# Loading the x tiles one stream at a time over 128 partitions, with new task lists

## The chip, the cores and the metric

The kernel runs on one core of one Trainium2 chip. The metric is device time in microseconds of one execution, without the host. The kernel before takes 252.27 us as the median of three runs (251.86 to 256.15). Lower is better.

A core has five engines that run side by side, each with its own instruction list: TensorE (PE in the profile, its weight loads PEld), VectorE (DVE), ScalarE (ACT), GpSimd (POOL) and SyncE (SP, which here only issues DMAs). DMAs are carried by 16 DMA engines, which all issuing engines share. Matmuls write to PSUM, which has 8 banks.

## The reference

One transformer layer in two halves, for one sequence of 2048 tokens with 448 features, in bfloat16.

```
h  = x + A(layernorm(x))
h2 = h + B(layernorm(h))

A: q,k,v = x @ wqkv, 16 heads of 28; each token attends to 8 keys,
   at distances 0, 2, 4, ... 14 before it; softmax; then @ wo
B: z = gelu(x @ w_in), split in z1 and z2 (896 each)
   g = w_sp @ layernorm(z2) + b_sp        (w_sp is 2048 x 2048)
   (z1 * g) @ w_out
```

## The kernel before

**Streams and tiles.** The 2048 tokens are cut into two streams of 1024 tokens, and the streams lie one over the other: a matmul with 64 rows serves stream 0, its partner in the other half of the array serves stream 1. For the attention, x is loaded in 9 tiles per stream. Tile i begins at token 114 i - 16 of its stream, so neighbouring tiles overlap by 14 tokens: the attention's look-back then stays inside a tile. Each tile has 128 tokens, the 64 even ones in partitions 0 to 63 and the 64 odd ones in partitions 64 to 127, since the attention looks back in steps of two. The first 16 tokens of tile 0 in stream 0 lie before the sequence and are set to zero.

**Where things lie.** The x tiles (`xs`) and the staged q weights share one buffer with a later stage; in the profile they are called z2p. The staged k and v weights lie in w_in. The padded copies of the q and k weights, the k and q results and several other tiles are views of `reg1`, `reg2`, `reg3`, which the profile shows as reg.

**Stages on TensorE.** First 15 matmuls on constant data, then transposes of the first tiles, q and k for tile 0 and for tile 1 (chunks 0 and 1), then tiles 2 to 4 together (chunk 2) and 5 to 8 together (chunk 3), with v, the logits, the row sums and the weighted sums of each tile in between; then the output projection (`mmy`), z2 and z1, and from about 132 us on the large product with w_sp (L1052) and the last product (L1081).

**A tile's way to TensorE.** Two loads; statistics on VectorE (`bn1`, lines 656 and 657, one pair of instructions per stream); the inverse deviation on ScalarE or GpSimd (`rs1`); normalization on VectorE (`nrm1`, line 674); then a transpose. Tiles 0 to 2 are transposed on TensorE (`tT1`), tiles 3 to 8 by a DMA (`tD1`, line 680) that SyncE issues.

**The loads.** Tile i is loaded by two DMAs, `xs i_0` for the even and `xs i_1` for the odd tokens (line 540). Each writes 64 partitions and takes both streams at once; tile 0 needs four smaller ones (lines 544 and 546). The source view has 64 rows outermost, then the two streams. The q, k and v weights come in four pieces each (line 559); q is copied by `cpq`, k by `cpk` into the padded form that the matmuls read. The loads of tiles 2 to 8 also wait until all four q pieces have landed (lines 587 to 589).

**What sets the order.** Every piece of work is a task with a modelled duration, dependencies and buffers. `SEQ` at the top of the file holds five lists of task numbers, one per engine, found beforehand by a search; `Planner.replay` walks them with the modelled durations, picks PSUM banks and buffers as it goes and emits the instructions in that order. At run time an engine runs its list strictly in order and waits on semaphores where the data needs it. So a modelled duration has no force at run time: it only decides which bank or buffer a task gets.

On SyncE the list of the kernel before begins with xs1_0, the pieces of tile 0, two q pieces, pieces of k and of the wo padding; then eight x loads; then the two large v pieces (wv0, wv1), more x loads and the transposes of tiles 3 and 4. ScalarE issues xs1_1, two q pieces, one k piece and one piece that serves k and v.

The functions that the change touches, with what calls them:

Of the kernel before, what the change touches and what calls it, by code (L numbers as in the profile page):

```python
# [6 lines left out]
D = 448  # L7
DH = 28
FH = 896
# [4 lines left out]
ST = 1024  # L14
# [20 lines left out]
SEQ = (  # L35
# [29 lines left out]
)  # L65
# [154 lines left out]
class Planner:  # L220
# [68 lines left out]
    def replay(self, t0=0.7):  # L289
# [13 lines left out]
        for _ in tasks:  # L303
# [34 lines left out]
            if t.nbytes:  # L338
                dma_free = max(dma_free, now + 0.3) + t.nbytes / t.bw / 1000.0
                t.end = dma_free + t.setup  # L340
                self.landed = max(self.landed, t.end)
            else:
                t.end = now + dur + extra
# [11 lines left out]
def bass_sequential_preLN__sliding_local_dilated__mixer_gmlp__prompt_kernel(  # L355
# [18 lines left out]
    with contextlib.ExitStack() as top:  # L374
# [101 lines left out]
        kv_old = r_wl["k"] + r_wl["v"]  # L476
        stg_old = r_wl["q"] + [r for i in range(NT) for s in range(2) for r in r_xs[i][s]]
        reg2_old = [r for rr in r_q + r_k for r in rr] + [r_qend]
# [26 lines left out]

        def dma(eng, name, fn, nbytes, deps=(), reads=(), writes=(), rel=(), store=False, issue=0.5, bw=245.0, after=(), setup=2.0):
            def em():
                rd = list(reads)
                for w in t.waits:
                    if w.nbytes:  # L510
                        rd.append(w.mark)
                    else:
                        rd += w.mark
                key, n = iss(eng, fn, reads=rd, writes=writes, prod="dma", inc=16, after=after)
                t.mark = Res("mark")
                t.mark.writes = {key: n}
                if store:
                    sch.store_keys.append(key)
            t = add(name, eng, issue, em, deps=deps, rel=rel, nbytes=nbytes)
            t.bw = bw  # L520
            t.setup = setup
            return t
# [10 lines left out]

        t_xs = [[] for _ in range(NT)]
        XT = X.rearrange("(s t) f -> t s f", s=2)

        def ld_xs(i, w, eng):
            lo = TQ * i - HALO + w
            if i:
                t_xs[i].append(dma(eng, "xs%d_%d" % (i, w), lambda e: e.dma_start(  # L540
                    xs[64 * w:64 * w + 64, i, :, :], XT[lo:lo + 127:2, :, :]), 128 * D * 2,
                    writes=[r_xs[i][0][w], r_xs[i][1][w]]))
                return
            t_xs[0].append(dma(eng, "xs0a_%d" % w, lambda e: e.dma_start(
                xs[64 * w + HALO // 2:64 * w + 64, 0, 0, :], X[w:w + 111:2, :]), 56 * D * 2, writes=[r_xs[0][0][w]]))
            t_xs[0].append(dma(eng, "xs0b_%d" % w, lambda e: e.dma_start(  # L546
                xs[64 * w:64 * w + 64, 0, 1, :], X[ST + lo:ST + lo + 127:2, :]), 64 * D * 2, writes=[r_xs[0][1][w]]))
        t_w = {}
# [7 lines left out]
        def ld_w(p, n, eng):  # L556
            c0 = "qkv".index(p[0]) * D
            dst, src = halves(w_st[p], A_wqkv[:, c0:c0 + D * len(p)])[n]
            t = dma(eng, "w%s%d" % (p, n), lambda e: e.dma_start(dst, src),
                    (64 if n > 1 else 384) * len(p) * D * 2, writes=[r_wl[x][n] for x in p], bw=200.0 if n > 1 else 330.0)  # L560
            for x in p:
                t_w.setdefault(x, []).append(t)
# [3 lines left out]
        def ld_win(z, deps, after=()):  # L566
            for n, (dst, src) in enumerate(halves(w_in[z], B_w_in[:, FH * z:FH * z + FH])):
                t = dma("sp", "win%d_%d" % (z, n), lambda e, dst=dst, src=src: e.dma_start(dst, src),
                        (64 if n > 1 else 384) * FH * 2, deps=deps, writes=[r_win[z][n]], bw=200.0 if n > 1 else 330.0, after=after)
                t_win.setdefault(z, []).append(t)  # L570
# [13 lines left out]
        for i in range(2, NT):  # L584
            ld_xs(i, 0, "sp")
            ld_xs(i, 1, "sp")
            for t in t_xs[i]:
                t.deps += t_w["q"]
                t.waits += t_w["q"]
        for n in range(4):  # L590
# [44 lines left out]
        def ln_unit(u, which, src_deps, after_h=()):  # L635
# [18 lines left out]
            for n in range(2):  # L654
                def em(n=n):
                    iss("dve", lambda e: e.bn_stats(st[n], src[n]), reads=rsrc[n], writes=[rl[n]])  # L656
                    iss("dve", lambda e: e.bn_aggr(mv[n], st[n]), reads=[rl[n]], writes=[rl[n]])  # L657
                tb.append(add("bn%d_%d_%d" % (which, u, n), "dve", 0.76, em, deps=src_deps))

# [26 lines left out]
            def em_t():  # L686
                o = bk[0] * 1024
                for c in range(NC7):
                    iss("pe", lambda e, c=c: e.transpose(psb[:, o + 128 * c:o + 128 * c + 128],
                                                        tring[:, h[0], 128 * c:128 * c + 128], ident[:, :]),  # L690
                        reads=r_tr[h[0]] + [r_ident], writes=[r_bank[bk[0]]])
            tt = add("tT%d_%d" % (which, u), "pe", 0.9 if u < 2 else 0.5, em_t, deps=tn + [c_ident], acq=[("ps", 1, bk)],
                     rel=[("tr", h)], mode="F", nmm=7)
# [10 lines left out]
        for i in range(NT):  # L704
            t_xh.append(ln_unit(i, 1, t_xs[i] + ([c_x0] if i == 0 else [])))

# [233 lines left out]
        for u in range(NU):  # L940
# [18 lines left out]
            t_h.append(th)  # L959
            t_hT.append(ln_unit(u, 2, [th]))  # L960
            tb3 = []
# [193 lines left out]
```

## Time and profile before

The profile is one execution on the chip, and its rows give microseconds.

| | |
|---|---|
| time, median of three runs | 252.27 us (251.86 to 256.15) |
| the profiled execution's own time | 255.13 us |
| its span, first to last instruction | 253.4 us |
| TensorE matmul, busy | 237.7 us (94%) |
| VectorE, busy | 138.3 us (55%) |
| ScalarE, busy | 86.7 us (34%) |
| GpSimd, busy | 23.4 us (9%) |
| mean clock granted to TensorE | 0.987 |
| moved by DMA | 25.62 MB, mean 101 GB/s |

How to read it: a row of a group names the line of the kernel, the engine, the operation, and the tiles written and read; then the count, the busy time, and the idle time before it with what ended it. "PE psum L802" is a matmul of line 802 that writes PSUM. A q or SPq names a queue or a DMA issue. In the views by time, the first number is the start in the span and the second the length. In a table of windows, the columns are the busy time of each engine, then the granted clock of TensorE, the mean busy share of the DMA engines, and GB/s.

### The profile page before, as it was taken

How to read it: one execution, taken by the hardware profiler on the slowest of the kernel's cores; microseconds unless marked ns; L12 is line 12 of the kernel's file. 1: busy time of each engine (PE TensorE's matmuls, PEld its weight loads, DVE VectorE, ACT ScalarE, POOL GpSimd, SP SyncE). 2: the span in 40 equal slices, each digit the busy share in tenths (PEclk: the TensorE clock that was granted, in tenths of full speed). 3: DMA queues.
4: the chain of work that ended last, by engine and by line, in shares of the span. 5: the costliest groups of instructions: out<-in, count | busy, mean ns of one | idle time of the engine just before them, and what ended most of it. 6: DMA issues, size and time to landing. Idle time of an engine off the chain costs nothing.

```text
span 253.4 us, 6573 instructions
## 1 busy us (share of the span) xinstructions
PE 237.7 (94%) x2942; PEld 119.5 (47%) x2952; DVE 138.3 (55%) x278; ACT 86.7 (34%) x110; POOL 23.4 (9%) x61
## 2 busy tenths in 40 slices
PE   7674999987999899999999999999999999999995
PEld 2372665544455454454444444444444444444443
DVE  3585975569599898769881005105700238321573
ACT  2543968676597834857571000000000000000000
POOL 7010200000030203203450000000000000000000
PEclk9997999999799999999999999999999999999999
DMA  5879987568863997695733363310000000010213
GB/s 153 238 189 203 259 97 184 81 106 117 171 169 54 209 221 180 120 131 119 160 84 85 83 153 79 77 26 0 3 0 0 18 0 21 0 36 0 75 36 110
DMA packets 60657, 25.62 MB, mean 101 GB/s; under 512 B 48084, under 2 KB 60484, under 8 KB 60628
## 3 DMA queue, kind: packets, MB, share of 16 engines
q1 hardware_dynamic: 59524, 24.22, 46.1%
q10 hardware_dynamic: 1104, 0.98, 1.4%
q8 instruction: 23, 0.38, 0.6%
q14 instruction: 6, 0.05, 0.1%
HBM read 11.75 MB, written 1.84 MB: 54 GB/s over the span
## 4 chain that ended last, share of the span: by engine, by line
PE 87%; DMA 5%; SPq 4%; issue 3%; DVE 0%
PE psum L1052 38%; PE psum L1081 8%; PE psum L1015 8%; PE psum L768 8%; PE psum L968 7%; PE psum L802 6%; PE psum L948 5%; PE psum L835 3%; SPq L540 3%; PE psum L891 2%; DMA z2p<-in_A_wqkv_dram 2%; DMA xh<-tring 2%; DMA w_in<-in_A_wqkv_dram 1%; PE psum L868 1%; SPq L546 1%
## 5 line engine op out<-in xcount | busy, mean ns | idle before, releaser
L1061 DVE TENSOR_TENSOR ub<-psum,reg 128x512 bf16<-128x512 f32 x28 | 18.8, 687 | 58.5 <-PE psum L1052 40.3
L1052 PE MATMUL psum<-reg,z2p 128*128 128x512 bf16 x219 | 49.2, 379 | 0.3
L1052 PE MATMUL psum<-wspT_lo,z2p 128*128 128x512 bf16 x219 | 48.7, 379 | 0.4 <-issue 0.2
L1052 PEld LDWEIGHTS psum<-wspT_lo,z2p 128*128 128x128 bf16 x224 | 21.8, 98 | 26.5 <-DVE z2p L998 0.4
L1052 PEld LDWEIGHTS psum<-reg,z2p 128*128 128x128 bf16 x224 | 21.8, 98 | 26.5 <-DVE ub L1061 0.4
L768 PE MATMUL psum<-xh,reg 64*128 64x114 bf16 (+3 forms) x448 | 27.2, 271 | 1.1 <-DVE reg L628 1.0
L968 PE MATMUL psum<-w_in,xh 64*128 64x448 bf16 x224 | 22.6, 349 | 0.4 <-DMA xh<-tring 0.4
L1081 PE MATMUL psum<-reg 128*128 128x448 bf16 (+1 forms) x119 | 22.3, 342 | 0.0
L1015 PE MATMUL psum<-xh,w_in 64*128 64x512 bf16 x196 | 22.0, 376 | 0.0
L626 ACT ACTIVATE reg<-psum 128x896 bf16<-128x896 f32 (+4 forms) x24 | 17.8, 758 | 11.0 <-PE psum L802 5.5
L1091 DVE TENSOR_TENSOR tring<-psum,x_tm 128x448 bf16<-128x448 f32 (+1 forms) x17 | 9.8, 594 | 21.1 <-PE psum L1081 21.1
L768 PEld LDWEIGHTS psum<-xh,reg 64*128 64x128 bf16 x448 | 16.3, 93 | 9.9 <-DVE reg L628 1.2
L802 PE MATMUL psum<-w_in,xh 64*128 64x448 bf16 x126 | 15.8, 398 | 4.3 <-issue 4.2
L984 DVE BATCH_NORM_STATS2 st<-z2p 128x6 f32<-128x448 bf16 x32 | 17.5, 611 | 3.2 <-ACT z2p L978 3.2
L850 ACT ACTIVATE reg<-psum 128x928 bf16<-128x928 f32 x18 | 16.4, 943 | 5.4 <-PE psum L835 5.2
L978 ACT ACTIVATE z2p<-psum 128x896 bf16<-128x896 f32 x16 | 13.9, 917 | 9.9 <-PE psum L968 6.5
L1025 ACT ACTIVATE reg<-psum 128x1024 bf16<-128x1024 f32 x14 | 13.9, 1029 | 7.9 <-PE psum L1015 7.9
L1081 PEld LDWEIGHTS psum<-reg 128*128 128x128 bf16 x119 | 11.5, 98 | 10.3 <-DVE tring L1091 0.4
L968 PEld LDWEIGHTS psum<-w_in,xh 64*128 64x128 bf16 x224 | 10.6, 94 | 11.2 <-DMA xh<-tring 0.8
L1015 PEld LDWEIGHTS psum<-xh,w_in 64*128 64x128 bf16 x196 | 9.5, 94 | 11.4
L631 POOL TENSOR_SCALAR rs<-mv 128x2 f32<-128x2 f32 x18 | 5.1, 284 | 105.0 <-DVE mv L657 86.0
L656 DVE BATCH_NORM_STATS2 st<-z2p 128x6 f32<-128x448 bf16 x18 | 11.0, 612 | 6.9 <-DMA z2p<-in_A_x_dram 6.8
(54 smaller groups left out, 202.8 us busy)
## 6 DMA issues: line engine op xcount, KB each, us to landing
w_in<-in_B_w_in_dram SPq DMA_DIRECT2D x4, 672.0 KB, 5.5
x_tm<-in_A_x_dram SPq DMA_DIRECT2D x4, 448.0 KB, 5.2
z2p<-in_A_x_dram SPq DMA_DIRECT2D x15, 112.0 KB, 3.3
out_dram<-tring SPq DMA_DIRECT2D x15, 112.0 KB, 1.8
w_in<-in_A_wqkv_dram SPq DMA_DIRECT2D x3, 336.0 KB, 5.8
reg<-in_A_wo_dram SPq DMA_DIRECT2D x4, 196.0 KB
reg<-in_B_w_out_dram SPq DMA_DIRECT2D x1, 784.0 KB, 5.6
reg<-in_B_b_sp_dram SPq DMA_DIRECT2D x1, 512.0 KB, 4.8
```

The costliest lines, as they stand in the source:

```text
L626: iss("act", lambda e: e.activation(dst, src, AF.Copy), reads=rd, writes=wr)
L768: iss("pe", lambda e, c=c, s=s, gi=gi, lhs=lhs, mov=mov: e.matmul(psum[:, bk[s] * 512 + cw * gi:bk[s] * 512 + cw * gi + cw], lhs, mov, sta ...
L802: iss("pe", lambda e, c=c, s=s: e.matmul(psum[:, bk[s] * 512:bk[s] * 512 + D], xh[64 * s:64 * s + 64, BLK[s][c], 128 * i:128 * i + 128], w ...
L850: iss("act", lambda e: e.activation(E[:, es[0], 2 * n:2 * n + 2, :], pair_view(lb, 0, 8 * JW), AF.Exp, scale=SCALE), reads=[r_bank[lb[0]], ...
L968: iss("pe", lambda e, c=c, s=s: e.matmul(psum[:, zb[s] * 512:zb[s] * 512 + D], xh[64 * s:64 * s + 64, BLK[s][c], 128 * u:128 * u + 128], w ...
L978: iss("act", lambda e: e.activation(z2p[:, u:u + 9:8, D * k:D * k + D], pair_view(zb, 0, D), AF.Gelu_apprx_tanh), reads=[r_bank[zb[0]], r_ ...
L984: iss("dve", lambda e, b=b: e.bn_stats(st3[:, b, k, :], z2p[:, b, D * k:D * k + D]), reads=[r_z2[b][k]], writes=[r_st3[b][k]])
L1015: iss("pe", lambda e, c=c, s=s: e.matmul(psum[:, bk[s] * 512:bk[s] * 512 + 512], w_in[0][64 * s:64 * s + 64, c, 128 * f:128 * f + 128], xh ...
L1025: iss("act", lambda e: e.activation(z1p[f].rearrange("p (s t) -> p s t", s=2)[:, :, 512 * ch:512 * ch + 512], pair_view(bk, 0, 512), AF.Ge ...
L1052: iss("pe", lambda e, b=b: e.matmul(psum[:, gb[0] * 512:gb[0] * 512 + 512], z2p[:, b, 128 * f:128 * f + 128], src[:, b, 512 * (tc % 2):512 ...
L1061: iss("dve", lambda e: e.tensor_tensor(ub[:, us_[0], :], psum[:, gb[0] * 512:gb[0] * 512 + 512], bb[:, 512 * tc:512 * tc + 512], ALU.add), ...
L1081: iss("pe", lambda e, f=f: e.matmul(psum[:, wb[0] * 512 + d0:wb[0] * 512 + d1], z1p[f][:, 128 * m:128 * m + 128], w_out[:, f, d0:d1], star ...
```

## The change

1. `ld_xs(i, n, eng)` now loads tile i of one stream n as one DMA over all 128 partitions. The source is a view that puts the parity w outermost (2), then the 64 rows of that parity. Tile 0 of stream 0, whose first rows are missing, is still loaded in two parts of 56 partitions. There are 17 full loads of 112 KB and these two parts, instead of 16 of 112 KB and four parts.
2. The loads of tiles 2 to 8 no longer wait for the q weights.
3. The statistics of one stream depend on that stream's load alone.
4. The model's constants change (issue of a DMA 0.62 instead of 0.5, all loads at 285 GB/s, start of a DMA 0.4, and others), and with them the five lists. There is one task less, so every number after it is shifted by one.

By name, SyncE now issues xs0_1, xs0_0b, xs1_0, xs0_0a, wk0, wop1, wkv3, wq3, xs2_1, xs2_0, wop0, xs3_1, wq1, wop2, xs4_1, wop3, xs3_0, xs4_0, wv1, wv0, xs8_1, xs8_0, xs6_0, xs7_0, xs5_1, xs7_1, xs6_1, then the transposes of tiles 4 and 3, then xs5_0 (here the second digit is the stream). ScalarE issues xs1_1, wkv2, wq2 and wk1, then runs rs1_1, then issues wq0. TensorE does k of tiles 1 and 0 first, then the transpose of tile 2, then q of tiles 0 and 1, then v of tiles 0, 2 and 1, the logits of tile 0, and chunk 2. VectorE takes the statistics of all loads in a new order; those of tile 6, stream 1 stand in its list ahead of the normalization of tile 6 and of `mask0`.

```diff
-        t_xs = [[] for _ in range(NT)]
-        XT = X.rearrange("(s t) f -> t s f", s=2)
-
-        def ld_xs(i, w, eng):
-            lo = TQ * i - HALO + w
-            if i:
-                t_xs[i].append(dma(eng, "xs%d_%d" % (i, w), lambda e: e.dma_start(
-                    xs[64 * w:64 * w + 64, i, :, :], XT[lo:lo + 127:2, :, :]), 128 * D * 2,
-                    writes=[r_xs[i][0][w], r_xs[i][1][w]]))
-                return
...
+        t_xs = [[[], []] for _ in range(NT)]
+
+        def ld_xs(i, n, eng):
+            lo = ST * n + TQ * i - HALO
+            if lo >= 0:
+                parts = [(xs[:, i, n, :], X[lo:lo + 128, :].rearrange("(j w) f -> w j f", w=2))]
+            else:
+                parts = [(xs[64 * w + HALO // 2:64 * w + 64, i, n, :], X[w:w + 111:2, :]) for w in range(2)]
+            for k, (dst, src) in enumerate(parts):
+                t = dma(eng, "xs%d_%d%s" % (i, n, "ab"[k] if len(parts) > 1 else ""), lambda e, dst=dst, src=src: e.dma_start(dst, src),
+                        128 * D * 2 // len(parts), writes=[r_xs[i][n][k]] if len(parts) > 1 else r_xs[i][n], bw=285.0)
+                t_xs[i][n].append(t)
...
             ld_xs(i, 0, "sp")
             ld_xs(i, 1, "sp")
-            for t in t_xs[i]:
-                t.deps += t_w["q"]
-                t.waits += t_w["q"]
...
-                tb.append(add("bn%d_%d_%d" % (which, u, n), "dve", 0.76, em, deps=src_deps))
+                tb.append(add("bn%d_%d_%d" % (which, u, n), "dve", 0.77, em, deps=src_deps[n]))
...
-            t_xh.append(ln_unit(i, 1, t_xs[i] + ([c_x0] if i == 0 else [])))
+            t_xh.append(ln_unit(i, 1, [t_xs[i][0] + ([c_x0] if i == 0 else []), t_xs[i][1]]))
```

More of the change, by code (lines that the diff above doesn't have):

```diff
@@ L338, in replay @@
             if t.nbytes:
-                dma_free = max(dma_free, now + 0.3) + t.nbytes / t.bw / 1000.0
+                dma_free = max(dma_free, now + 0.4) + t.nbytes / t.bw / 1000.0
                 t.end = dma_free + t.setup
@@ L476, in bass_sequential_preLN__sliding_local_dilated__mixer_gmlp__prompt_kernel @@
         kv_old = r_wl["k"] + r_wl["v"]
-        stg_old = r_wl["q"] + [r for i in range(NT) for s in range(2) for r in r_xs[i][s]]
+        stg_old = r_wl["q"] + [r for i in range(NT) for rr in r_xs[i] for r in rr]
         reg2_old = [r for rr in r_q + r_k for r in rr] + [r_qend]
@@ L504, in dve4x, with dma @@
             return (190.0 + 0.26 * n) / 1000.0
-        def dma(eng, name, fn, nbytes, deps=(), reads=(), writes=(), rel=(), store=False, issue=0.5, bw=245.0, after=(), setup=2.0):
+        def dma(eng, name, fn, nbytes, deps=(), reads=(), writes=(), rel=(), store=False, issue=0.62, bw=285.0, after=(), setup=2.0):
             def em():
@@ L532, in ld_x @@
                 t_x[b] = t
-        t_xs = [[] for _ in range(NT)]
-        XT = X.rearrange("(s t) f -> t s f", s=2)
-        def ld_xs(i, w, eng):
-            lo = TQ * i - HALO + w
-            if i:
-                t_xs[i].append(dma(eng, "xs%d_%d" % (i, w), lambda e: e.dma_start(
-                    xs[64 * w:64 * w + 64, i, :, :], XT[lo:lo + 127:2, :, :]), 128 * D * 2,
-                    writes=[r_xs[i][0][w], r_xs[i][1][w]]))
-                return
[L544 to L547, printed above, removed]
+        t_xs = [[[], []] for _ in range(NT)]
[9 more added lines that the diff above has]
+                t_xs[i][n].append(t)
         t_w = {}
@@ L559, in ld_w @@
             t = dma(eng, "w%s%d" % (p, n), lambda e: e.dma_start(dst, src),
-                    (64 if n > 1 else 384) * len(p) * D * 2, writes=[r_wl[x][n] for x in p], bw=200.0 if n > 1 else 330.0)
+                    (64 if n > 1 else 384) * len(p) * D * 2, writes=[r_wl[x][n] for x in p], bw=285.0)
             for x in p:
@@ L568, in ld_win @@
                 t = dma("sp", "win%d_%d" % (z, n), lambda e, dst=dst, src=src: e.dma_start(dst, src),
-                        (64 if n > 1 else 384) * FH * 2, deps=deps, writes=[r_win[z][n]], bw=200.0 if n > 1 else 330.0, after=after)
+                        (64 if n > 1 else 384) * FH * 2, deps=deps, writes=[r_win[z][n]], bw=285.0, after=after)
                 t_win.setdefault(z, []).append(t)
@@ L691, in em_t @@
                         reads=r_tr[h[0]] + [r_ident], writes=[r_bank[bk[0]]])
-            tt = add("tT%d_%d" % (which, u), "pe", 0.9 if u < 2 else 0.5, em_t, deps=tn + [c_ident], acq=[("ps", 1, bk)],
+            tt = add("tT%d_%d" % (which, u), "pe", 0.55, em_t, deps=tn + [c_ident], acq=[("ps", 1, bk)],
                      rel=[("tr", h)], mode="F", nmm=7)
@@ L959, in bass_sequential_preLN__sliding_local_dilated__mixer_gmlp__prompt_kernel @@
             t_h.append(th)
-            t_hT.append(ln_unit(u, 2, [th]))
+            t_hT.append(ln_unit(u, 2, [[th], [th]]))
             tb3 = []
```

58 rows, old and new, of the table SEQ are left out of this document.

## The prediction

> **What bounds the kernel now.** I read the page's first part, then the chain that ended last, then TensorE's and SyncE's timelines over the first 30 us, where the change works, then the DMA issues and the windows. The page:
>
> ```profile
> span 253.4 us, 6573 instructions
> ...
> PE 237.7 (94%) x2942; PEld 119.5 (47%) x2952; DVE 138.3 (55%) x278; ACT 86.7 (34%) x110; POOL 23.4 (9%) x61
> ...
> PE 87%; DMA 5%; SPq 4%; issue 3%; DVE 0%
> ```
>
> TensorE is the bound, and its work stays the same. So only its stalls can move the time. The chain in order of time (start, length, what):
>
> ```profile
> 4.99 4.53 DMA z2p<-in_A_wqkv_dram
> ...
> 9.53 0.03 SPq L176
> ...
> 15.63 3.58 DMA w_in<-in_A_wqkv_dram
> 19.21 3.04 issue
> 22.26 2.73 PE psum L802 x14
> ...
> 32.33 1.32 PE psum L802 x14
> ...
> 53.66 0.95 issue
> ...
> 61.88 1.30 issue
> ...
> 86.12 0.95 issue
> ```
>
> The chain runs through loads until 22.26. A q piece lands at 9.52, SyncE stops waiting for it at 9.53, x loads follow, and a v piece issued at 15.63 heads the last wait before the first product with v (L802). After that it is TensorE, with 0.95 + 1.30 + 0.95 = 3.2 us of small stalls. TensorE's timeline around the gap:
>
> ```profile
> 10.42 1.82 PE L768 MATMUL psum<-xh,reg 64*128 64x114 bf16 x56
> 13.26 4.83 PE L768 MATMUL psum<-xh,reg 64*128 64x114 bf16 x168 [1.02 <-DVE reg L628]
> 22.26 2.73 PE L802 MATMUL psum<-w_in,xh 64*128 64x448 bf16 x14 [4.17 <-issue]
> ...
> 29.06 3.26 PE L768 MATMUL psum<-xh,reg 64*128 64x342 bf16 x42
> ```
>
> q and k of tiles 0 and 1 end at 18.09, then 4.17 us of idling for the v pieces. Chunk 2 (tiles 2 to 4) starts at 29.06. I call that start **S**: both lists do the same tasks on TensorE ahead of it (18 by count), and the same work up to the last output projection behind it. The change is worth what it does to S, plus what later stalls change.
>
> ```profile
> 6.56 0.47 SPq L559 DMA_DIRECT2D w_in<-in_A_wqkv_dram x1
> 9.60 5.99 SPq L540 DMA_DIRECT2D z2p<-in_A_x_dram x8
> 15.63 1.13 SPq L559 DMA_DIRECT2D w_in<-in_A_wqkv_dram x2
> ...
> 21.82 1.33 SPq L680 DMA_TRANSPOSE xh<-tring x1
> ```
>
> SyncE stands still from 7.03 to 9.60. This is the wait that the change removes, and behind it are queued eight x loads, both v pieces and the transposes of tiles 3 and 4.
>
> **The change part by part.** *The removed wait* frees 2.6 us of SyncE, and the issue count is nearly the same (19 x loads instead of 20; 5.99 / 8 = 0.75 us a load). By the issues alone, 18 of them at some 0.6 us from 0.8 on, the v pieces go out at about 11.5 instead of 15.63. What decides is how fast the loads land:
>
> ```profile
> z2p<-in_A_x_dram SPq DMA_DIRECT2D x15, 112.0 KB, 3.3
> ...
> w_in<-in_A_wqkv_dram SPq DMA_DIRECT2D x3, 336.0 KB, 5.8
> reg<-in_A_wo_dram SPq DMA_DIRECT2D x4, 196.0 KB
> ...
> xh<-tring SPq DMA_TRANSPOSE x14, 3.7
> ...
> z2p<-in_A_x_dram SPq DMA_DIRECT2D x2, 56.0 KB, 4.2
> reg<-in_A_wo_dram SPq DMA_DIRECT2D x4, 28.0 KB
> ...
> out_dram<-tring SPq DMA_DIRECT2D x2, 56.0 KB, 1.8
> z2p<-in_A_x_dram SPq DMA_DIRECT2D x2, 49.0 KB
> ```
>
> The last figure is the time to landing. Three rows have none: the pieces of 28 partitions (196 KB), of 4 (28 KB) and of 56 (49 KB). All loads whose outermost count is 64 or 128 have one. So a load is dealt out by its outermost count, and a count that 16 doesn't divide leaves some of the 16 DMA engines without a share, so that no full set of landings is seen. **The new x load** has 128 rows outermost on the side it writes, but its source view `w j f` has **2** outermost. No row shows such a load. From one side it runs on all 16 engines like its 112 KB neighbours (3.3 us to landing), from the other on two, with 64 rows of 896 bytes each. I take two, since the three rows without landing are the ones that show what an outermost count does. The Trainium skill, "DMA: Bandwidth & Descriptors", section "Why a DMA increments its semaphore by 16 and not by 1", states it as a rule: the slowest dimension of each side that isn't 1 is taken, the engine count is the largest up to 16 that divides both, and the lowest-numbered engines are used. By it, 56, 28 and 4 partitions give 14, 14 and 4, which fits the three rows, and 128 against 2 gives two engines, the same two each time.
>
> *Price of a row on one engine:*
>
> ```profile
> 2.00:13.00 11.00, 8.29 (x88) 4.05 (x86) 5.37 (x14) 5.30 (x8) 3.25 (x13) 1.00 0.83 232
> 9.00:10.00 1.00, 0.12 (x2) 0.12 (x3) 0.88 (x3) 1.00 (x3) 0.00 (x0) 1.00 1.04 363
> 19.00:20.00 1.00, 0.00 (x0) 0.00 (x0) 0.97 (x4) 0.93 (x3) 0.00 (x0) 1.00 1.00 320
> 22.00:25.50 3.50, 3.24 (x20) 1.67 (x21) 1.48 (x5) 0.48 (x1) 0.00 (x0) 0.55 1.10 197
> ```
>
> ```profile
> q10 hardware_dynamic: 1104, 0.98, 1.4%
> ```
>
> At a busy share of 1.00 the engines moved 320 GB/s, 20 GB/s each: 44.8 ns for 896 bytes. Bounds are 39.5 ns (363 GB/s) and, by ScalarE's queue, 1.4% of 16 x 253.4 us over 1104 packets, 51 ns.
>
> *The sum to S.* Ahead of the transposes of tiles 3 and 4 the lists have 16 full x loads (all but xs5_0). On each of the two engines that is 16 x 64 = 1024 rows, 45.9 us. The weights in front of them are spread over 16 engines and put a sixteenth on these two: 6 pieces of 336 KB, two of 112, two of 56, so 147 KB, 7.5 us. The four wo paddings put a 7 KB row each, 1.4 us, and tile 0's two parts 0.4. Together 55.2 us. The DMAs start to move at about 2.2, so the pair is through at 57.4. The transposes stand behind in the same queue. They have long been issued by then, so I add the shortest landing that the rows show, 1.8, and 0.3 for the second one: S = 59.5, or **+30.4 us**.
>
> *What hides it:* nothing. TensorE has q, k and v of the first tiles and one set of logits, some 12 us of work, and runs out while x is still landing. *The wait that the change adds* is the one of VectorE for xs6_1, the last load of the 16: behind it in VectorE's list stand five more statistics, the normalizations of tiles 5 to 8 and `mask0`.
>
> ```profile
> L656 DVE BATCH_NORM_STATS2 st<-z2p 128x6 f32<-128x448 bf16 x18 | 11.0, 612 | 6.9 <-DMA z2p<-in_A_x_dram 6.8
> ```
>
> At about 0.75 us a statistics pair, `mask0` ends near 63.5 and tile 8's normalization near 66, so its transpose lands near 71. TensorE comes to chunk 3 about 12 us behind S, at 71.5. That is level, so I take 0 (up to 4 if it slips). *The clock:* after the 4.17 us gap it was granted 0.55 over 3.5 us, and the 14 matmuls of L802 took 2.73 instead of 1.32. The new gap comes on top, so +1.4. *The small stalls* of 3.2 us lie where short matmuls follow each other densely. The new list has about as many such places: 0, up to 1 either way. *Statistics per stream, k ahead of q, wq0 behind rs1_1, the new constants:* 0, since all lie ahead of S in the shadow of the loads; without that cover they are worth at most the 1.02 us that TensorE waits at 13.26. Behind S the lists differ in order, not in work: 0, up to 3 either way.
>
> Sum: 30.4 + 1.4 = **+31.8 us**. The profiled execution's own time, 255.13 (its span of 253.4 and 1.7 around it), becomes 286.9. The median shown is 252.27, 2.9 lower, so the forecast is **284**.
>
> **The rivals.**
>
> *All 16 engines carry it (the other side: faster).* Against it stand the rows without landing, for it that the written side has 128 rows. Up to the last k piece 1414 KB are then ahead; at the 232 GB/s of 2 to 13 us they are there near 8.5, landed near 9.2, copied by 10.0. TensorE's first q and k product starts there instead of at 10.42, and its 1.82 + 4.83 us, one tile's transpose of 0.6 and up to 0.9 for the q pieces bring it to 18. The v pieces end 3570 KB, moved by 18.0 and landed near 18.6: a gap of 0.6. Three products of 1.32 and 0.6 for logits give S = 23.2, 5.9 less, of which I take 1 back for new stalls: **247.4**, range 244 to 253. It holds if the new loads land in under 5 us. The Trainium skill, same page, "Rules for kernel authors", speaks for this one: two transfers to disjoint halves of the partitions don't gain, one over 128 partitions is better. The 3.3 us of the present 64-partition loads beside the 5.8 of weights over 128 show no such loss.
>
> *Two engines, but another pair each time.* Then a load takes 64 x 44.8 ns = 2.9 us instead of an eighth of that, and eight run side by side. The first statistics come 2.5 us late and S is 25.7, a gain of 3.4 less 1 for stalls: **249.9**. Against it: the 4-partition pieces in the queue all leave some engines out, and nothing in the rows suggests a turn.
>
> **How the numbers follow.** Two engines, always the same: 0.82, 284. All 16: 0.13, 247.4. Turning pairs: 0.05, 249.9. Own range of the first: by 39.5 ns the 55.2 become 48.7, so 277.5; by 51 ns 62.8, so 291.7. Two engines that don't compete with 14 others may run faster than any row shows (a quarter more than 44.8 ns allows gives 273); less the clock's 1.4, stalls and lists that is 268. Above, 4 us at chunk 3 and 2 us of longer landing make 298. So **268 to 298** holds about 0.98 of 0.82, 0.8 in all, and the other cases are left out. 2% is 5 us, about what a measurement of this kernel can tell from no change. Slower by over 2%: 0.82. The second case lies at the border of -2%, so its 0.13 goes half to faster, and the turning pairs lie mostly within: within 2% 0.10, faster 0.08.
>
> **What would show it.** Right: the x loads of 112 KB have no landing time in the table of issues; between 10 and 55 us the DMA share is under 0.3 and the rate near 40 to 60 GB/s; the statistics (L656) wait for x loads for tens of us; chunk 2 (64x342) starts at 53 to 67 after a long gap, and behind it TensorE is as dense as before. Wrong, for the second case: landings of 3 to 5 us, no gap ahead of L802, chunk 2 near 23. If chunk 2 starts late but the DMA share is high, the reason is another one.

## The result and the profile after

The changed kernel takes 281.47 us (median of four runs, 280.12 to 282.87), the kernel before beside it 253.8 us: a ratio of 1.1119, with a 95% interval of 1.0995 to 1.1242. The forecast of 284 was 2.5 us too high, inside its range. The profiled execution took 282.87 us, 27.7 more than that of before. Here and below a time is the median of all executions, and a ratio leaves out those that are over 1.5% longer than the fastest of the same kernel.

The page of the changed kernel: its span, the busy time of the engines, the shares of the chain that ended last, and the statistics on VectorE (L651 here, L656 before).

```profile
span 280.8 us, 6563 instructions
...
PE 243.4 (87%) x2941; PEld 125.4 (45%) x2952; DVE 137.4 (49%) x277; ACT 87.3 (31%) x111; POOL 24.9 (9%) x61
...
PE 56%; SPq 20%; DMA 13%; DVE 7%; issue 2%; ACT 1%; POOL 0%; DVEq 0%
...
L651 DVE BATCH_NORM_STATS2 st<-z2p 128x6 f32<-128x448 bf16 x18 | 11.1, 615 | 35.8 <-DMA z2p<-in_A_x_dram 35.8
```

TensorE fell from 94% busy to 87%. On the chain, SyncE's queue went from 4% to 20% and DMA from 5% to 13%. The statistics waited 6.8 us for x loads before, and wait 35.8 now.

Its DMA issues, with the time to landing at the end of a row where there is one:

```profile
z2p<-in_A_x_dram SPq DMA_DIRECT2D x16, 112.0 KB
...
w_in<-in_A_wqkv_dram SPq DMA_DIRECT2D x3, 336.0 KB, 7.7
...
xh<-tring SPq DMA_TRANSPOSE x14, 4.5
```

The 112 KB x loads have lost their landing time, as the rows of 4, 28 and 56 partitions had none before.

The chain from 28 to 56 us (start, length, what):

```profile
28.49 2.93 SPq L543
31.42 0.04 issue
31.46 2.25 SPq L543
...
36.13 2.33 SPq L543
...
38.50 2.33 SPq L543
...
40.88 2.33 SPq L543
...
43.25 4.42 SPq L675
...
47.73 2.31 SPq L675
...
50.08 6.15 DMA z2p<-in_A_x_dram
```

SyncE issued an x load in 0.75 us before. Here an issue takes 2.33 us from 33.76 us on, and the issues follow each other almost without a break: SyncE itself is held up by the queue that it fills. The two transposes behind the loads (L675) are issued at 43.25 and 47.73 only. The steady 2.37 us from start to start is the time in which the queue drains one load.

TensorE's timeline (start, length, line; in brackets the idle time before it and what ended it):

```profile
34.91 6.06 PE L797 MATMUL psum<-w_in,xh 64*128 64x448 bf16 x42 [5.33 <-ACT xh L621]
40.90 0.70 PE L830 MATMUL psum<-reg 32*64 32x58 bf16 x64
52.23 7.09 PE L763 MATMUL psum<-xh,reg 64*128 64x342 bf16 x70 [10.63 <-DMA xh<-tring]
...
66.41 2.92 PE L763 MATMUL psum<-xh,reg 64*128 64x456 bf16 x28
```

Chunk 2 starts at S = 52.23 instead of 29.06, after 10.63 us of waiting for a transposed tile. Chunk 3 follows at 66.41 without a wait. The windows (busy time of PE, PEld, DVE, ACT, POOL, then granted clock, DMA share, GB/s):

```profile
30.00:40.00 10.00, 5.09 (x34) 2.55 (x36) 3.63 (x10) 3.87 (x8) 2.11 (x7) 0.66 0.15 50
40.00:50.00 10.00, 1.60 (x76) 0.91 (x70) 0.81 (x2) 2.38 (x3) 0.00 (x0) 0.78 0.59 61
...
52.00:56.00 4.00, 3.77 (x28) 2.37 (x30) 2.44 (x8) 0.75 (x1) 1.50 (x6) 0.51 0.93 219
```

From 30 to 40 us, where SyncE issues only x loads, the 16 engines are busy for 0.15 of the time and move 50 GB/s. Two engines of 16 are 0.125. At 52 to 56 the granted clock is 0.51.

The semaphores in the traces count the engines directly. An x load's semaphore gets 3 marks here, where one of the kernel before gets 16, and a wo padding of 4 partitions gets 5 in both kernels. That is one mark for each engine, and below 16 engines one more, which comes soon after the issue. The load issued at 33.76 has its two late marks at 42.99 and 43.24, the next one at 45.39 and 45.66, the one after it at 47.80 and 48.06. So the loads land one after the other, though three are under way: from 32 to 43 us 2.2 of their rows are moving at a time on average. Three loads on three different pairs would have six moving, so it is the same pair each time.

The span grew by 27.4 us: 23.2 ahead of S, and 4.2 behind it (228.6 us from S to the end, 224.3 before).

### The profile page after: what moved, and what is told of

Same layout as the page of the kernel before. It is cut to its first block, busy times and chain, and to the rows that moved or that the text cites. A ratio compares the mean times of both kernels' runs of the same rounds, so it can differ in the third digit from the quotient of the medians.

```text
span 280.8 us, 6563 instructions
## 1 busy us (share of the span) xinstructions
PE 243.4 (87%) x2941; PEld 125.4 (45%) x2952; DVE 137.4 (49%) x277; ACT 87.3 (31%) x111; POOL 24.9 (9%) x61
## 4 chain that ended last, share of the span: by engine, by line
PE 56%; SPq 20%; DMA 13%; DVE 7%; issue 2%; ACT 1%; POOL 0%; DVEq 0%
PE psum L1047 30%; SPq L543 9%; PE psum L1076 8%; DMA reg<-in_B_w_sp_dram 7%; PE psum L763 5%; PE psum L943 5%; SPq L675 3%; PE psum L797 3%; SPq L915 3%; SPq L557 2%; DMA z2p<-in_A_x_dram 2%; PE psum L830 2%; DMA reg<-in_B_b_sp_dram 2%; DVE st L651 2%; SPq L925 2%
## 5 line engine op out<-in xcount | busy, mean ns | idle before, releaser
L763 PE MATMUL psum<-xh,reg 64*128 64x114 bf16 (+3 forms) x448 | 30.3, 298 | 11.4 <-DMA xh<-tring 10.6
L763 PEld LDWEIGHTS psum<-xh,reg 64*128 64x128 bf16 x448 | 19.6, 106 | 20.8 <-issue 12.4
L651 DVE BATCH_NORM_STATS2 st<-z2p 128x6 f32<-128x448 bf16 x18 | 11.1, 615 | 35.8 <-DMA z2p<-in_A_x_dram 35.8
L621 ACT ACTIVATE reg<-psum 128x684 bf16<-128x684 f32 (+4 forms) x25 | 18.2, 756 | 22.1 <-PE psum L763 18.3
L963 PE MATMUL psum<-w_in,xh 64*128 64x448 bf16 x224 | 22.4, 349 | 0.5 <-DMA xh<-tring 0.4
L797 PE MATMUL psum<-w_in,xh 64*128 64x448 bf16 x126 | 17.3, 429 | 5.3 <-ACT xh L621 5.3
```

Of the source, the lines that this page charges most:

```text
L621: iss("act", lambda e: e.activation(dst, src, AF.Copy), reads=rd, writes=wr)
L763: iss("pe", lambda e, c=c, s=s, gi=gi, lhs=lhs, mov=mov: e.matmul(psum[:, bk[s] * 512 + cw * gi:bk[s] * 512 + cw * gi + cw], lhs, mov, sta ...
L797: iss("pe", lambda e, c=c, s=s: e.matmul(psum[:, bk[s] * 512:bk[s] * 512 + D], xh[64 * s:64 * s + 64, BLK[s][c], 128 * i:128 * i + 128], w ...
L963: iss("pe", lambda e, c=c, s=s: e.matmul(psum[:, zb[s] * 512:zb[s] * 512 + D], xh[64 * s:64 * s + 64, BLK[s][c], 128 * u:128 * u + 128], w ...
```

## The experiments

The theory is that the two rows outermost in the source view put each x load on two DMA engines, always the same, and that this alone makes the kernel slow. The rivals are that the new lists or the removed wait do it, or that one DMA over 128 partitions is itself the slow form. The kernel before took 253.58 us beside `dose16`, `dose4`, `parity` and `halves`, and 254.68 beside `dose8`, `view`, `tfirst` and `nowait`.

### The number of rows outermost: 4, 8, 16

```diff
-                parts = [(xs[:, i, n, :], X[lo:lo + 128, :].rearrange("(j w) f -> w j f", w=2))]
+                parts = [(xs[:, i, n, :], X[lo:lo + 128, :].rearrange("(j w) f -> w j f", w=16))]
```

(w=4 and w=8 in the other two.) Lists, bytes, rows and instructions stay those of the changed kernel.

> The changed kernel with one number altered: the source view of a full x load has 16 outermost instead of 2. It is still one DMA per stream over 128 partitions, with the same lists and waits. The tokens of a tile land in another order, so the attention mixes other tokens and the output isn't the reference's; the work is the same. Theory A (a load runs on as many DMA engines as its outermost count allows): the x loads get a landing time again, under 5 us; chunk 2 starts at 23 to 25 us instead of 52.23, and the time is 246 to 252. Rival B (the new lists and the missing wait flood the DMA queue or starve TensorE): chunk 2 stays past 40, the time 270 or more. Rival C (one DMA over 128 partitions with interleaved rows is slow by itself): x landings of tens of us and a time of 275 to 285.

> As the kernel with 16 outermost, but with 4 (again the tokens of a tile are in another order and the output isn't the reference's). Theory A: no landing time for the x loads, four engines with 32 rows a load at the 36.4 ns that the changed kernel shows (2.33 us for 64 rows), so SyncE issues late x loads every 1.2 us; 16 loads take 18.6 us, with the weights' share of about 6, the paddings' 1.4 and 2.2 to begin with 28.5 us, and chunk 2 starts at 30 to 33; the time is 252 to 259. Rivals B and C: no difference to the changed kernel, 275 to 285.

> Edit: the changed kernel with 8 outermost in the source view instead of 2. The tokens of a tile then lie in another order, so another function is computed, with the same instructions. Theory A (the outermost count sets the number of DMA engines, 36.4 ns a row of 896 bytes on each): 16 rows on each of 8 engines, 0.58 us a load, 9.3 us for 16 loads, below what the weights and the issues need. Chunk 2 starts at 26 to 30 (2 gave 52.23, 4 gave 37.91, 16 gave 25.08) and the time is 252 to 257 us; no landing time if a full set of 16 landings is what the table wants, and a landing time if it wants less. Rival (a load is either on all engines or on a fixed few): 265 to 281.

Measured: 252.31 us for 16 (ratio to before 0.9926, 0.9859 to 0.9994), 254.06 for 8 (0.9954, 0.9908 to 1.0001), 265.02 for 4 (one run). With 16, the DMA issues and TensorE's timeline:

```profile
z2p<-in_A_x_dram SPq DMA_DIRECT2D x16, 112.0 KB, 5.4
```

```profile
25.08 5.34 PE L763 MATMUL psum<-xh,reg 64*128 64x342 bf16 x70
```

With 8, the same views:

```profile
z2p<-in_A_x_dram SPq DMA_DIRECT2D x16, 112.0 KB
```

```profile
28.14 5.34 PE L763 MATMUL psum<-xh,reg 64*128 64x342 bf16 x70
```

With 4, SyncE's timeline (the second row is the last four of the seven loads of the first) and TensorE's:

```profile
19.61 8.94 SPq L543 DMA_DIRECT2D z2p<-in_A_x_dram  x7
...
23.95 4.60 SPq L543 DMA_DIRECT2D z2p<-in_A_x_dram  x4
```

```profile
37.91 6.98 PE L763 MATMUL psum<-xh,reg 64*128 64x342 bf16 x70 [4.00 <-DMA xh<-tring]
```

So S is 52.23, 37.91, 28.14 and 25.08 for 2, 4, 8 and 16. The marks on an x load's semaphore are 3, 5, 9 and 16. The landing time is there for 16 alone; its absence therefore says "fewer than 16 engines" and not "slow". The same seven x loads take 15.58 us to issue with two engines (27.63 to 43.21) and 8.94 with four. Halving the rows per engine from 64 to 32 about halves the steady time of a load too, from 2.37 to 1.15 (4.60 / 4): 36 to 37 ns a row in both. The rule of the Trainium skill's "DMA: Bandwidth & Descriptors", section "Why a DMA increments its semaphore by 16 and not by 1", by which the slowest dimensions of the two sides set the number of engines, agrees with these four points.

The expectation for 4 was missed: chunk 2 came at 37.91, not at 30 to 33, and the time was 265.02, not 252 to 259. The last of the 16 loads landed at 34.48 in the trace, where the sum had 28.5, and chunk 2 began 3.4 us behind it. From 3.3 us on there are never fewer than four packets under way, so no gap in the queue shows; why the work ahead of the steady stretch took longer than the sum is open. The numbers for 16 were missed by little (5.4 us to landing and not under 5, S at 25.08 and not by 25, 252.31 and not by 252), and those for 8 came true. The rivals had 270 us or more for 16, 275 for 4 and 265 for 8, so the series rules them out for 16 and 8, and the single run with 4 lies 10 us below theirs.

### The same lists with loads of 64 partitions

`parity` takes back the loads of before (64 partitions, both streams), and keeps the new lists and the missing wait. `halves` keeps one load per stream, but cuts it into two DMAs of 64 partitions:

```diff
-                parts = [(xs[:, i, n, :], X[lo:lo + 128, :].rearrange("(j w) f -> w j f", w=2))]
+                t_xs[i][n].append(dma_n(eng, "xs%d_%d" % (i, n), [lambda e, w=w: e.dma_start(
+                    xs[64 * w:64 * w + 64, i, n, :], X[lo + w:lo + w + 127:2, :]) for w in range(2)], ...
```

> The changed kernel with the x loads of before (64 partitions, both streams, 64 rows outermost) for tiles 1 to 8, and tile 0 of stream 1 in two loads of 64 rows; new lists, no wait for the weights. The output is the reference's. Theory A: chunk 2 starts at 23 to 25.5 (statistics of a stream now need both loads of the tile, and there is one issue more), time 246 to 252. Rival B: 270 or more, since lists and waits are those of the changed kernel. Rival C: 246 to 252, like A, so this run separates B alone.

> The changed kernel with each full x load of a stream cut in two DMAs of 64 partitions with 64 rows outermost, issued one behind the other; new lists, no wait for the weights, statistics per stream. The output is the reference's. Theory A: all engines, but 17 issues more at 0.4 to 0.6 us, nine of them ahead of the v pieces, which go out near 16 and land near 21: chunk 2 at 25 to 29, time 249 to 255. Rival B: 270 or more.

`parity`: 255.12 us, ratio 1.0063 (0.9998 to 1.0129). Its TensorE timeline has chunk 2 at 28.20:

```profile
28.20 5.34 PE L782 MATMUL psum<-xh,reg 64*128 64x342 bf16 x70
```

The new lists and the missing wait without the new view cost nothing that can be told from zero, so rival B falls. The expected gain (chunk 2 at 23 to 25.5, 246 to 252 us) did not come either; what takes it was not tried. `halves`: 260.8, ratio 1.0351 (1.025 to 1.0452). SyncE's and TensorE's timelines of `halves`:

```profile
18.10 9.32 SPq L548 DMA_DIRECT2D z2p<-in_A_x_dram  x14
27.47 3.32 SPq L686 DMA_TRANSPOSE xh<-tring  x2
```

```profile
32.60 7.03 PE L774 MATMUL psum<-xh,reg 64*128 64x342 bf16 x70 [6.22 <-DMA xh<-tring]
```

Twice the issues at 0.67 us each push the transposes to 27.47, where the 16-engine loads of `dose16` have them at 20.00, and S to 32.60 instead of 25.08. The expectation of 249 to 255 had counted the issues ahead of the v pieces, which do go out at 15.94, but not the seven more ahead of the transposes, and at 0.4 to 0.6 us each. The Trainium skill, "DMA: Bandwidth & Descriptors", section "Rules for kernel authors", prefers one 128-partition transfer to two of half the partitions. With 16 engines at work on both, 25.08 against 32.60, this case agrees, here by the issues, and the changed kernel shows that the view's outermost count goes before it.

### The view alone in the kernel before

```diff
-                    xs[64 * w:64 * w + 64, i, :, :], XT[lo:lo + 127:2, :, :]), 128 * D * 2,
-                    writes=[r_xs[i][0][w], r_xs[i][1][w]]))
+                    xs[:, i, w, :], X[...].rearrange("(j w) f -> w j f", w=2)), 128 * D * 2,
+                    writes=r_xs[i][w]))
```

> Edit: the kernel before, with its own task lists and its wait for the q weights, where only the x loads of tiles 1 to 8 are changed: each takes one stream over 128 partitions through the view with the parity outermost (2). Theory A (two DMA engines carry every such load, 2.33 us a load): from 9.6 us on 13 loads stand ahead of the first transpose, 30.3 us, with some 3 us of weights on the same two engines and 2 to landing; chunk 2 starts at 46 to 50 and the time is 268 to 276 us. No landing time in the table of issues. Rival B (the new lists and the removed wait make the change slow, and the view is worth little): chunk 2 starts at 28 to 31 and the time is 250 to 256.

282.05 us (two runs), ratio 1.1113 (1.103 to 1.1197): the whole of the change's loss, with the old lists and the old wait. SyncE's timeline and TensorE's:

```profile
12.56 15.19 SPq L540 DMA_DIRECT2D z2p<-in_A_x_dram  x8
27.79 3.21 SPq L559 DMA_DIRECT2D w_in<-in_A_wqkv_dram  x2
```

```profile
36.93 2.80 PE L802 MATMUL psum<-w_in,xh 64*128 64x448 bf16 x14 [13.77 <-DMA w_in<-in_A_wqkv_dram]
...
55.06 4.97 PE L768 MATMUL psum<-xh,reg 64*128 64x342 bf16 x42 [10.79 <-DMA xh<-tring]
```

Chunk 2 starts at 55.06, outside the expected 46 to 50, and the time is above the 268 to 276. The expectation let the loads begin at 9.6, where they begin in the kernel before. But tile 1's loads lie on the two engines ahead of the q pieces, these land later, and the wait now ends at 12.56. The rest lies with the second transpose. In the chain, an x load issued at 37.39 lands at 47.3, its statistics and normalization release the transpose at 48.12, and this takes 6.82 us to land, where the expectation had 2. In the trace, pieces of wo (landed at 50.88 and 51.02) and one more x load (53.96) come ahead of it. Behind S this kernel takes 223.8 us, about as the kernel before (224.3).

### The transposes ahead of the last x loads

In the changed kernel, SyncE's list alone, by names:

```diff
-xs7_0, xs5_1, xs7_1, xs6_1, tD1_4, tD1_3, xs5_0
+xs7_0, tD1_4, tD1_3, xs5_1, xs7_1, xs6_1, xs5_0
```

> Edit: the changed kernel, with only SyncE's list altered: the transposes of tiles 4 and 3 stand ahead of the last three x loads (xs5_1, xs7_1, xs6_1) instead of behind them. Theory A (the transposes come late because SyncE is held by the queue while it issues the loads ahead of them, 2.33 us each): they are issued three loads earlier, chunk 2 starts at 44 to 46 instead of 52.23, and VectorE, which waited for chunk 2's sums in PSUM before it normalized tiles 5 to 8, comes earlier as well; time 274 to 277 us. Rival (the loads of tiles 5 to 8 set when chunk 3 can start, and that is not earlier): chunk 2 at 44 to 46, but the products of chunk 3 (64x456) again near 66 us, and the time 279 to 282.

282.64 us, ratio 1.1141 (1.1096 to 1.1187): the transposes come earlier and nothing is gained. TensorE's timeline, and ScalarE's and VectorE's:

```profile
46.31 7.71 PE L763 MATMUL psum<-xh,reg 64*128 64x342 bf16 x70 [5.28 <-DMA xh<-tring]
60.99 0.58 PE L863 MATMUL psum<-reg,ones 64*32 64x464 bf16 x8 [6.97 <-ACT reg L621]
...
69.52 2.92 PE L763 MATMUL psum<-xh,reg 64*128 64x456 bf16 x28
```

```profile
58.84 0.29 ACT L661 ACTIVATE rs<-mv,epst 128x2 f32<-128x2 f32 x1 [7.57 <-DVE mv L652]
...
60.13 1.98 ACT L621 ACTIVATE reg<-psum 128x684 bf16<-128x684 f32 x3
```

```profile
54.02 0.63 DVE L651 BATCH_NORM_STATS2 st<-z2p 128x6 f32<-128x448 bf16 x1 [12.27 <-DMA z2p<-in_A_x_dram]
```

Chunk 2 starts 5.9 us earlier, and then TensorE waits 6.97 for ScalarE. ScalarE stands at the inverse deviation of tile 5 (L661), with the copies out of PSUM (L621) queued behind it. It needs the statistics of xs5_0, and these stand in VectorE's list behind those of xs6_1 and four others. xs6_1 arrives at 54.0, and from there VectorE works through its list without a break to 58.8. Everything queued behind those statistics, on VectorE and ScalarE, moves with that load. So the 2.33 us a load is paid at chunk 2 or just behind it. The theory's 274 to 277 falls. The rival's 279 to 282 is near (282.64), and its reason is only half right: chunk 3 comes even later than in the changed kernel (69.52 instead of 66.41), and not just the transposes of tiles 5 to 8, but already the results of chunk 2 wait.

### The removed wait by itself

```diff
-            for t in t_xs[i]:
-                t.deps += t_w["q"]
-                t.waits += t_w["q"]
```

in the kernel before.

> Edit: the kernel before, without the wait of the x loads of tiles 2 to 8 for the q weights, all else as before. Theory A (SyncE stands still for 2.6 us and the v pieces stand behind it): the v pieces are issued some 2.5 us earlier, the gap ahead of the first product with v shrinks from 4.17 us to 1 to 2.5, chunk 2 starts at 26.5 to 28, time 250 to 252.5 where the kernel before has 253.6. Rival (how fast the 16 engines move the bytes decides, not when they are issued): chunk 2 starts at 28.5 to 29.5 and the time is that of before within 1 us.

250.65 us (249.82 to 255.45, five runs), ratio 0.9862 (0.982 to 0.9905). SyncE's timeline and TensorE's:

```profile
7.06 5.18 SPq L540 DMA_DIRECT2D z2p<-in_A_x_dram  x8
12.28 1.14 SPq L559 DMA_DIRECT2D w_in<-in_A_wqkv_dram  x2
```

```profile
20.43 1.50 PE L799 MATMUL psum<-w_in,xh 64*128 64x448 bf16 x14 [1.68 <-issue]
...
26.82 3.28 PE L765 MATMUL psum<-xh,reg 64*128 64x342 bf16 x42 [0.90 <-DMA xh<-tring]
```

The v pieces go out at 12.28 instead of 15.63, the gap ahead of the first product with v is 1.68 instead of 4.17, and chunk 2 starts at 26.82 instead of 29.06. The theory's numbers hold, but for the v pieces, which go out 3.35 us earlier and not 2.5. This is the one part of the change that gains by itself, and this kernel is faster than both the one before (by about 1.4%) and the changed one. Together with the new lists, in `parity`, the gain is not there.

## Why the prediction was right

**Two engines, always the same.** Right. The number is shown by the marks and by the series 2, 4, 8, 16, and the same pair by the loads that land one after the other. The rows without a landing time were the right ones to read.

**The price of a row.** This is the mis-sized term. 44.8 ns were taken from a time in which all 16 engines were busy, with 39.5 and 51 as bounds. The steady 2.37 us a load over 64 rows is 37.0 ns, below the lower bound. The 16 loads' 45.9 us become 37.9, and the weights' 7.5 become 6.2 at the same rate. By the prediction's own sum (37.9 + 6.2 + 1.4 + 0.4 + 2.2) the pair would be through at 48.1. VectorE's timeline has the last of the 16 loads there at 50.48:

```profile
50.48 0.63 DVE L651 BATCH_NORM_STATS2 st<-z2p 128x6 f32<-128x448 bf16 x1 [8.77 <-DMA z2p<-in_A_x_dram]
```

That is 2.4 us more than the sum. No gap in the queue shows: from 3 us until then there are never fewer than two packets under way. A mean of 39 ns a row would make it up; why rows ahead of the steady stretch should take longer was not tried.

**The landing of the transposes.** "They have long been issued by then" failed: they were issued at 43.25 and 47.73, since SyncE is held by the queue. The sum survived it narrowly: the second issue ended at 50.04, the loads were done at 50.48, and chunk 2 began 1.8 us later, where 1.8 and 0.3 had been forecast. S came at 52.23 instead of 59.5.

**VectorE's added wait at 0.** Right for this list order, by a narrow margin: chunk 3 starts at 66.41 without a wait, 14.2 us behind S, and TensorE waits 0.15 us for a copy of VectorE at 59.47. `tfirst` shows the wait that it covers: 5.9 us less at chunk 2 give 6.97 of waiting behind it. The prediction had named VectorE's queue (the statistics, normalizations and `mask0` behind xs6_1). It had missed that ScalarE's list has inverse deviations ahead of copies out of PSUM.

**The clock, +1.4.** The 70 matmuls of chunk 2 at the start took 7.09 us, and 5.34 in `dose16`, so 1.75.

**Behind S, 0 up to 3 either way.** 4.2 us were lost there, 1.75 of them to the clock, which the sum carried as a term of its own. The new lists may account for 1.8 of the rest: `dose16` and `dose8` take 226.1 us from S to the end of the span (251.2 - 25.08 and 254.2 - 28.14), the kernel before 224.3, and the view with the old lists 223.8. But these are single profiles, executions of one kernel differ by more than this (248.82 to 254.85 for `dose16`), and `view` loses 1.7 to the clock too (42 matmuls in 4.97 us instead of 3.26) without taking longer behind S. So how the rest divides is not shown.

**The sum.** +31.8 was forecast and +27.7 measured. At S it was 7.2 us too high: 9.3 by the row price, less some 2 that the loads took longer than the sum at the right price. Behind S it was some 2.8 too low. That 284 came within 2.5 us is therefore partly luck: with rows at 37.0 ns and all else as forecast it would have been 274.7, 6.8 too low, and still in the range.

**The rival with all 16 engines.** Its price was too good: `dose16`, which is that case, has S at 25.08 and not 23.2, and takes 252.31 and not 247.4. Of its 4 us at S little is left in the whole. So "faster by over 2%" would not have come true even then.

**What would show it.** The missing landing time, waits of tens of us at the statistics and a long gap ahead of chunk 2 came true; its start, 52.23, lies just ahead of the 53 to 67. The share and the rate held only from 30 to 46 us (0.15 at 50 GB/s). From 10 to 30 us, with the weights in the queues, they were 0.35 to 0.38 at 108 to 116 GB/s. From 46 to 50 the share was 1.25 at 77 GB/s: the first packets of the transposes (256 bytes) start at 46.23 in the trace, and some of them are recorded as under way for up to 3.6 us, which the share counts. The rate is the safer reading there.

## What to carry to other kernels

Before a load is rearranged, look at the outermost count of both of its sides, not only at the number of partitions: a view that puts a 2 outermost cost 11% here with every byte and instruction kept. A load without a landing time in the table of issues is the sign of it. And a transfer that waits for nothing can still hold up its issuing engine, and with it every transfer queued behind it; try such an edit apart from what it is bundled with, as the removed wait here gained 1.4% alone and nothing together with the new lists.

## What the runs showed beside that

**The issuing engine is held at a certain depth.** In the steady stretch SyncE's issue of a load with two engines ends when the load three before it has landed (43.21 and 43.24 in the trace), so three loads, 192 rows on each engine, are under way. With four engines it is five loads, 160 rows. Below that an issue takes 0.65 us (5.18 / 8 in `nowait`). What sets the depth was not tried.

**A gap of 1.3 to 1.6 us cost about its length again in the clock, and one of 0.95 us did not.** In the profile of `nowait` (an execution of 255.45 us) TensorE waits 1.61 us with nothing to wait for, then runs at half the clock:

```profile
49.21 1.49 PE L799 MATMUL psum<-w_in,xh 64*128 64x448 bf16 x14
...
60.32 0.38 PE L832 MATMUL psum<-reg 32*64 32x58 bf16 x12 [1.61 <-issue]
60.62 2.80 PE L799 MATMUL psum<-w_in,xh 64*128 64x448 bf16 x14
```

```profile
60.30:62.00 1.70, 1.68 (x20) 0.84 (x21) 0.83 (x3) 1.26 (x2) 0.00 (x0) 0.50 0.09 22
...
63.70:65.40 1.70, 1.70 (x74) 0.92 (x69) 0.33 (x1) 0.68 (x1) 0.00 (x0) 1.00 0.87 256
```

The same 14 matmuls take 2.80 us behind the gap and 1.49 elsewhere: 1.31 on top of 1.61. The kernel before has gaps of both kinds:

```profile
54.62 0.24 PE L891 MATMUL psum<-reg 64*32 64x58 bf16 x14 [0.95 <-issue]
...
63.18 0.29 PE L835 MATMUL psum<-reg 32*64 32x58 bf16 x12 [1.30 <-issue]
63.40 2.79 PE L802 MATMUL psum<-w_in,xh 64*128 64x448 bf16 x14
```

```profile
54.00:56.00 2.00, 1.38 (x84) 1.08 (x85) 1.29 (x2) 0.79 (x2) 0.00 (x0) 1.00 0.09 22
...
64.00:65.00 1.00, 1.00 (x8) 0.44 (x6) 0.56 (x2) 1.00 (x2) 0.00 (x0) 0.50 0.20 50
```

Behind the gap of 0.95 us the clock stays at 1.00; behind that of 1.30 it is 0.50, and the 14 matmuls take 2.79. The prediction had priced the small stalls by their length alone. What causes such gaps, which lie where short matmuls follow each other densely, was not settled.
